# Hashed attention and two MLPs on one core: hash in 32-column tiles, bits through DRAM, values in threes

## The chip, the cores and the metric

One core of one Trainium2 chip. The metric is the device time of one execution in microseconds (us). The engines are named as in the profile: PE (TensorE matmul), PEld (its weight loads), DVE (VectorE), ACT (ScalarE), POOL (GpSimd) and SP (SyncE, which here only issues DMAs).

## The reference

Sixteen heads (2 x 8) of 768 queries and keys, 64 features each. A query attends to a key only where six sign bits of a projection agree. Two MLPs follow (1536 tokens, 512 to 2048 to 512).

```python
q_bits = (np.einsum('bhsd,dk->bhsk', q, proj) > 0)      # k_bits alike, 6 bits
mask = q_bucket[:, :, :, None] == k_bucket[:, :, None, :]
scores = np.where(mask, scale * np.matmul(q, k.transpose(0, 1, 3, 2)), -1e9)
attn = np.exp(scores - max); attn = attn / (sum + 1e-9)
x = np.matmul(attn, v)                                  # then to 1536 x 512
h = x @ w_in;  g = softplus(h);  x = g @ w_out          # MLP 1
h = x @ w_in;  g = h * clip(h + 3, 0, 6) / 6;  out = g @ w_out   # MLP 2
```

## The kernel before

The program is written by a planner (`Schedule`). Each `plan.add` names an operation, its planned cost on each engine that may run it, the buffers it reads and writes, and a priority (lower goes first). `Schedule.run` then plays the program forward on a model of the engines: at each step it takes the engine whose next operation would end first, and gives that engine the operation with the lowest priority among those that can start soonest. The order in which it emits the instructions is the order in which each engine's queue executes them on the chip. So every constant of the planner (`TH`, `WHEN`, `STAY`, `START`, `EVERY`, `STEP`, `PROJECT`, `ACTIVATE`, `FETCH`, `AHEAD`) changes only orders, and the choice of engine where an operation may run on two.

`prepare(h)` loads a head and builds its operands. The tile `raw` holds k on partitions 0 to 63 and q on 64 to 127. `qa`, `ka` are rounded parts, `qb`, `kb` the remainders (64 rows) with 32 rows of bits below them (`KB` = 96): q's bits and ones, k's bits and -2^33, so that the product of `qb` and `kb` also counts bit mismatches as a large penalty. `dot` (L379) multiplies `raw` by the signed projection `hashes`, in two matmuls of 64 output columns and 384 keys that stand side by side in the array, into one PSUM bank `d`; L401 compares it with 0 on all 128 partitions (`bt`, 128x384), and four DMAs (L410) carry 32 rows each from `bt` to `qb` and `kb`. For head 0, DVE writes the bits to `qb`/`kb` itself (L391, four instructions of 32 rows).

`attend(h)` runs six query blocks `t`. For each: four score matmuls (L437 with `qa`/`ka`, L438 with `qb`/`kb`) into a two-bank PSUM tile `sc`; the maximum over keys on DVE (L451); a tiny DVE instruction that makes bias and scale (L458); exp on ACT with a row sum (L466); six PE transposes to `tp` (L477), and their copy to `et` (L249 on ACT or L251 on DVE; DVE may have it where `t % 3` is 0). `sc` and `tp` share three two-bank tiles. The product with v (`some(c)`, L493) has six key blocks `c`, each two 64-column matmuls side by side; they are planned as three operations of two blocks. Each such fp32 matmul stands in the trace as two instructions, so a head has 24 rows of L493 and 4 of L379. `xa`, `pt` (L515), `xn`, and per two heads `xt` (L557), `xh`, `xl` bring the result to the MLP's layout. `d`, `av`, `pt` and `xt` share two single PSUM banks ("av", "pre"). During attention one block of MLP weights per head is also converted from 64-bit floats, on ACT and DVE (L600 to L643); its earliest start is `START + EVERY * n`.

The MLPs (L662 hidden, L755/L757 output) are 2304 matmuls of 512 columns on PE.

Of the kernel before, what the change touches and what calls it, by code (L numbers as in the profile page):

```python
# [9 lines left out]
F32 = mybir.dt.float32  # L10
# [21 lines left out]
LATER = 4  # L32
BITS = 3
EX = 3

TH = 16.41
WHEN = dict(load_p=-69.22, load_k=-58.24, load_q=23.18, load_v=-47.14, high_k=64.04, high_q=79.83, low_k=32.38, low_q=105.41, copy_q=116.1, dots=124.52, bits=46.23, send=11.13, scores=-1.98, max=-149.65, exp=-149.76, turn=-8.77, even=-56.85, values=53.65, back=58.37, rec=72.46, norm=75.82, x=27.98, x_high=21.57, x_low=7.85)
# [11 lines left out]
STEP = 8.253  # L49
PROJECT = 11.022  # L50
ACTIVATE = -66.584
FETCH = 125.921
AHEAD = -20.863


def f32(ap):
# [28 lines left out]
class Schedule:  # L85
# [24 lines left out]
    def run(self):  # L110
        free = dict(A=1.96, D=0.1, P=0.6, T=0.1, S=0.65, H=0.0, G=0.0, M=0.0)
        lanes, busy, mode = [0.0] * LANES, {}, "r"
        ready = {op: self.times(op) for op in self.ops if not op.open}
        while ready:
            options = []
            for op, times in ready.items():
                slot = self.slots(op)
                if slot is not None:
                    for e, t in times.items():
                        at, end, unit = max(free[e], slot, t), op.cost[e], e  # L120
                        if e == "T":
# [5 lines left out]
                        options.append((op.prio, at, at + end, unit, e, op))  # L127
# [8 lines left out]
            _, start, end, _, e, op = min(rivals, key=lambda o: (late(o), o[1]))  # L136
# [24 lines left out]
        assert all(op.done is not None for op in self.ops)  # L161
        return max(free.values())
# [30 lines left out]
def lsh_attention_two_mlps(  # L193
# [37 lines left out]
    for name in ("x", "w", "bits"):  # L231
        open_pool(name, ctx)
    open_pool("ps", ctx, space=PSUM)
    open_pool("tail", attention, side="right")
    open_pool("heads", heads)

# [26 lines left out]
    thr = buffer("heads", [P, 1], F32, "thr", 1, "thr")  # L263
    top = buffer("heads", [P, 1], F32, "top", 1, "top")

    def set_rows(e):

        for u in range(P // ROWS):
            bounds = ((0.0, NB), (-TINY, NR), (0.0, P)) if u % 2 == 0 else ((-TINY, NB), (0.0, P))
            rows = thr.ap[u * ROWS : (u + 1) * ROWS, :]  # L270
            for i, (value, _) in enumerate(bounds):
                if i == 0:
                    nc.gpsimd.memset(rows, value)
                else:
                    nc.gpsimd.affine_select(
                        out=rows, in_=rows, compare_op=ALU.is_gt, fill=value, base=bounds[i - 1][1],
                        pattern=[[0, 1]], channel_multiplier=-1,
                    )
            nc.gpsimd.memset(top.ap[u * ROWS : (u + 1) * ROWS, :], -BIG if u % 2 else 1.0)
# [17 lines left out]
    plan.add(dict(D=0.6), set_hashes, reads=[p32], writes=[hashes], prio=-39)  # L297


    qa, qb, ka, kb, vx = {}, {}, {}, {}, {}  # L300

    def prepare(h):
        at = h * TH
# [77 lines left out]
                    start=True, stop=True,  # L381
                )

        plan.add(dict(T=0.646), dot, mode="c", reads=[raw, hashes], writes=[dots], prio=at + WHEN["dots"])
        if h == 0:
            for u in range(2):
                for n, x in enumerate((qb, kb)):
                    rows = slice((2 * u + n) * ROWS, (2 * u + n + 1) * ROWS)
                    plan.add(
                        dict(D=0.6),  # L390
                        lambda e, u=u, x=x, rows=rows: nc.vector.tensor_scalar(  # L391
                            x[h].ap[D:KB, u * HALF : (u + 1) * HALF], dots.ap[rows, :HALF], thr.ap[rows, 0:1],
                            top.ap[rows, 0:1], op0=ALU.is_gt, op1=ALU.mult,
                        ),
                        reads=[dots, thr, top], writes=[x[h]], prio=at + WHEN["bits"],
                    )
            return
        bits = buffer("heads", [P, HALF], F32R, "bt", 2, f"bt{h}")
        plan.add(
            dict(D=0.585),  # L400
            lambda e: nc.vector.tensor_scalar(  # L401
                bits.ap, dots.ap[:, :HALF], thr.ap[:, 0:1], top.ap[:, 0:1], op0=ALU.is_gt, op1=ALU.mult
            ),
            reads=[dots, thr, top], writes=[bits], prio=at + WHEN["bits"],
        )
        for u in range(2):
            for n, x in enumerate((qb, kb)):
                plan.add(
                    queue,
                    lambda e, u=u, n=n, x=x: engines[e].dma_start(  # L410
                        out=f32(x[h].ap[D:KB, u * HALF : (u + 1) * HALF]),
                        in_=f32(bits.ap[(2 * u + n) * ROWS : (2 * u + n + 1) * ROWS, :]),
                    ),
                    reads=[bits], writes=[x[h]], prio=at + WHEN["send"], dma=(0.2, 1.95),
                )


    xn = {}
# [1 line left out]
    def attend(h):  # L420
# [19 lines left out]
        for t in range(NT):  # L440
# [3 lines left out]
            for u in range(2):  # L444
                last_scores = plan.add(
                    dict(T=0.353), lambda e, sc=sc, t=t, u=u: scores(sc, t, u),
                    reads=[qa[h], qb[h], ka[h], kb[h]], writes=[sc], prio=step + WHEN["scores"],
                )
            plan.add(
                dict(D=0.866),  # L450
                lambda e, sc=sc, t=t: nc.vector.reduce_max(  # L451
                    nm.ap[:, t, 0:1], sc.ap[:, :, :HALF], axis=AX.XY, negate=True
                ),
                reads=[sc], writes=[nm], prio=step + WHEN["max"],
            )
            plan.add(
                dict(D=0.07),
                lambda e, t=t: nc.vector.scalar_tensor_tensor(  # L458
                    bs.ap[:, t, :], nm.ap[:, t, 0:1].to_broadcast([P, 2]), 0.5 * BIG, nm.ap[:, t, :],
                    op0=ALU.is_lt, op1=ALU.mult,  # L460
                ),
                reads=[nm], writes=[bs], prio=step + WHEN["max"],
            )
# [17 lines left out]
            def even(e, tp=tp, t=t):  # L481
# [399 lines left out]
```

## Time and profile before

| | |
|---|---|
| time, median of 3 | 787.0 us (785.72 to 787.37) |
| profiled execution: its own time | 787.35 us |
| its span, first to last instruction | 785.6 us |
| granted PE clock, mean | 0.998 |
| busy: PE, PEld, DVE, ACT | 764.9, 599.1, 529.0, 485.0 us |

A matmul row's length runs to the modelled end of its pipeline and overlaps the next; the distance between the starts of neighbouring rows is the time that PE gives to each. A row of the chain is time on the path that ended last.

### The profile page before, as it was taken

How to read it: one execution, taken by the hardware profiler on the slowest of the kernel's cores; microseconds unless marked ns; L12 is line 12 of the kernel's file. 1: busy time of each engine (PE TensorE's matmuls, PEld its weight loads, DVE VectorE, ACT ScalarE, POOL GpSimd, SP SyncE). 2: the span in 40 equal slices, each digit the busy share in tenths (PEclk: the TensorE clock that was granted, in tenths of full speed). 3: DMA queues.
4: the chain of work that ended last, by engine and by line, in shares of the span. 5: the costliest groups of instructions: out<-in, count | busy, mean ns of one | idle time of the engine just before them, and what ended most of it. 6: DMA issues, size and time to landing. Idle time of an engine off the chain costs nothing.

```text
span 785.6 us, 10356 instructions
## 1 busy us (share of the span) xinstructions
PE 764.9 (97%) x3808; PEld 599.1 (76%) x3808; DVE 529.0 (67%) x938; ACT 485.0 (62%) x821; POOL 9.5 (1%) x53
## 2 busy tenths in 40 slices
PE   4999999999999999999999999999999999999997
PEld 2677677677668788878888788878888888888886
DVE  6698887888986999964545899999932222232222
ACT  3789999998988778665556678766622322232222
POOL 1000000000000000000000000000000000000000
PEclk9999999999999999999999999999999999999999
DMA  5354454353323070000000555530000100010001
GB/s 165 108 162 116 115 165 120 110 163 118 80 73 134 28 294 1 1 0 1 1 0 1 188 196 191 177 107 1 1 0 14 42 0 1 1 53 1 1 0 54
DMA packets 26354, 58.61 MB, mean 75 GB/s; under 512 B 3584, under 2 KB 7552, under 8 KB 26304
## 3 DMA queue, kind: packets, MB, share of 16 engines
q1 hardware_dynamic: 22128, 49.56, 19.7%
q10 hardware_dynamic: 4176, 8.39, 3.4%
q8 instruction: 30, 0.49, 0.3%
q14 instruction: 20, 0.16, 0.1%
HBM read 48.89 MB, written 3.15 MB: 66 GB/s over the span
## 4 chain that ended last, share of the span: by engine, by line
PE 90%; ACT 4%; DVE 3%; issue 2%; DMA 1%; SPq 0%; ACTq 0%; DVEq 0%
PE ph L662 34%; PE acc L755 17%; PE acc L757 17%; PE tp L477 7%; PE av L493 6%; PE sc L437 4%; PE sc L438 3%; ACT e L466 2%; DVE nm L451 2%; PE xt L557 1%; ACT ka L249 1%; PE pt L515 1%; PE d L379 1%; DMA raw<-in_q_dram 1%; ACT et L249 0%
## 5 line engine op out<-in xcount | busy, mean ns | idle before, releaser
L662 PE MATMUL ph<-xh,w 128*128 128x512 f32 x768 | 239.1, 393 | 0.0
L662 PEld LDWEIGHTS ph<-xh,w 128*128 128x128 f32 x768 | 143.8, 188 | 31.7
L662 PE MATMUL ph<-xl,w 128*128 128x512 f32 x384 | 150.2, 391 | 0.0
L691 DVE SCALAR_TENSOR_TENSOR ml<-me,ph 128x512 f32<-128x512 f32 x48 | 33.1, 690 | 116.0 <-ACT me L686 115.8
L686 ACT ACTIVATE me<-ph,three 128x512 f32<-128x512 f32 x48 | 33.0, 687 | 124.2 <-PE ph L662 120.7
L466 ACT ACTIVATE e<-sc,bs 128x768 f32<-128x768 f32 x96 | 94.0, 986 | 19.0 <-DVE bs L458 19.0
L451 DVE TENSOR_REDUCE nm<-sc 128x1 f32<-128x768 f32 x96 | 88.7, 951 | 20.8 <-PE sc L438 20.6
L755 PE MATMUL acc<-gh,w 128*128 128x512 f32 x384 | 98.8, 395 | 0.1
L757 PE MATMUL acc<-w,gh 128*128 128x512 f32 x384 | 97.4, 392 | 0.0
L477 PEld LDWEIGHTS tp<-ident,e 128*128 128x128 f32 x576 | 63.3, 142 | 29.3 <-ACT e L466 20.2
L755 PEld LDWEIGHTS acc<-gh,w 128*128 128x128 f32 x384 | 70.9, 188 | 19.1 <-ACT gh L249 2.8
L757 PEld LDWEIGHTS acc<-w,gh 128*128 128x128 f32 x384 | 72.1, 188 | 16.2
L662 PEld LDWEIGHTS ph<-xl,w 128*128 128x128 f32 x384 | 72.1, 188 | 16.0
L477 PE MATMUL tp<-ident,e 128*128 128x128 f32 x576 | 76.6, 281 | 4.9 <-ACT e L466 3.8
L437 PE MATMUL sc<-ka,qa 128*128 128x384 f32 x192 | 69.1, 360 | 0.1
L493 PE MATMUL av<-et,vx 128*64 128x384 f32 x384 | 68.8, 494 | 0.0
L438 PE MATMUL sc<-kb,qb 96*128 96x384 f32 x192 | 65.3, 340 | 0.8 <-DVE kb L391 0.7
L249 ACT ACTIVATE et<-tp 128x768 f32<-128x768 f32 x82 | 62.2, 815 | 2.4 <-PE tp L477 2.3
L722 DVE SCALAR_TENSOR_TENSOR me<-mu,me 128x512 f32<-128x512 f32 x48 | 33.3, 693 | 33.1 <-ACT mu L717 33.0
L249 ACT ACTIVATE gh<-ml 128x512 fp32r<-128x512 f32 x48 | 30.2, 629 | 38.8 <-DVE ml L734 38.6
L755 PE MATMUL acc<-gl,w 128*128 128x512 f32 x192 | 53.4, 392 | 0.7 <-ACT xh L249 0.7
L757 PE MATMUL acc<-w,gl 128*128 128x512 f32 x192 | 53.1, 391 | 0.0
(65 smaller groups left out, 957.8 us busy)
## 6 DMA issues: line engine op xcount, KB each, us to landing
raw<-in_moe_w_out_dram SPq DMA_DIRECT2D x30, 512.0 KB, 3.5
raw<-in_moe_w_in_dram SPq DMA_DIRECT2D x18, 512.0 KB, 4.3
raw<-in_moe_w_in_dram ACTq DMA_DIRECT2D x14, 512.0 KB, 4.8
rawk<-in_kv_dram SPq DMA_DIRECT2D x15, 384.0 KB, 5.0
raw<-in_kv_dram SPq DMA_DIRECT2D x16, 192.0 KB, 3.2
raw<-in_q_dram SPq DMA_DIRECT2D x16, 192.0 KB, 3.7
vx<-in_kv_dram SPq DMA_DIRECT2D x16, 192.0 KB, 3.0
out_dram<-y SPq DMA_DIRECT2D x12, 256.0 KB, 2.1
```

The lines of the kernel that those rows point to most:

```text
L249: nc.scalar.activation(out, in_, AF.Copy)
L437: nc.tensor.matmul(o, qa[h].ap[:, qs], ka[h].ap[:, cs], start=True, stop=False)
L438: nc.tensor.matmul(o, qb[h].ap[0:KB, qs], kb[h].ap[0:KB, cs], start=False, stop=True)
L451: lambda e, sc=sc, t=t: nc.vector.reduce_max(nm.ap[:, t, 0:1], sc.ap[:, :, :HALF], axis=AX.XY, negate=True),
L466: lambda e, sc=sc, ex=ex, t=t: nc.scalar.activation(ex.ap.rearrange("p (u k) -> p u k", u=2), sc.ap[:, :, :HALF], AF.Exp, bias=bs.ap[:, t, ...
L477: nc.tensor.transpose(o, ex.ap[:, c * P : (c + 1) * P], ident.ap)
L493: nc.tensor.matmul(av.ap[u * D : (u + 1) * D, :HALF], vx[h].ap[:, c, :], et[u].ap[:, c, :], start=(c == 0), stop=(c == NT - 1),)
L662: nc.tensor.matmul(bank(), w[:, a, :], x[b].ap[:, kc, :], start=(kc + i == 0), stop=(kc == KC - 1 and i == 2))
L691: lambda e: nc.vector.scalar_tensor_tensor(l.ap, e1.ap, 6.0, bank(), op0=ALU.min, op1=ALU.mult),
L722: lambda e: nc.vector.scalar_tensor_tensor(e1.ap, u.ap, -1.0, e1.ap, op0=ALU.add, op1=ALU.subtract),
L755: nc.tensor.matmul(o, w.ap[:, a, cs], b.ap, start=st, stop=sp)
L757: nc.tensor.matmul(o, b.ap[:, cs], w.ap[:, a, :], start=st, stop=sp)
```

## The change

- The hash of heads 1 to 15 is four matmuls (`dot4`) of 32 output columns and 192 keys, one for each quarter of the keys, side by side, with `hash4` as weights. The comparison is one instruction on 128x192 (planned 0.386 for 0.585), with threshold columns `thr4`, `top4` of its own. The bit rows in `qb` and `kb` shrink from 32 to 16 (`KB` = 80).
- The bits go to `qb` and `kb` through a DRAM tile `sent`: one DMA writes it, two read it (before: four DMAs within SBUF).
- Head 0 keeps the old hash; its four bit writes are four planned operations in the order q0, k0, k1, q1, and a score matmul waits only for the halves that it reads.
- POOL builds `thr4`, `top4` (28 small instructions) and `hash4` (three) at the start.
- Maximum and bias of a query block are one planned operation, so L458's successor follows its maximum at once on DVE.
- The copy of `tp` may go to DVE for every `t`.
- The products with v are two planned operations of three key blocks (before: three of two).
- The planner adds `LEAN` (0.731 us) to DVE's end when it compares engines for an operation that two may run, and `LOOK`: an operation of lower priority number may be taken although it can start only up to 0.412 us (ACT), 0.103 (DVE) or 0.108 (PE) later than the soonest one.
- All constants have new values.

```diff
-TH = 16.41
+GROUP = 3
+TH = 14.059
-STAY = 10.971
+STAY = 48.452
+LEAN = 0.731
+LOOK = dict(A=0.412, D=0.103, T=0.108)
-START, EVERY = 33.82, 14.426
+START, EVERY = 19.12, 13.251
...
-            end, unit = min((o[2], o[3]) for o in options)
+            end, unit = min((o[2] + o[6], o[3]) for o in options)
...
-            rivals = [o for o in rivals if o[1] <= soon]
+            rivals = [o for o in rivals if o[1] <= soon + LOOK.get(unit, 0.0)]
...
-    KB = D + ROWS
+    BR = ROWS // 2
+    KB = D + BR
+    QT = S // 4
...
+    def set_quarters(e):
+        for u in range(P // ROWS):
+            rows = slice(u * ROWS, (u + 1) * ROWS)
+            steps(thr4.ap[rows, :], ((0.0, NB), (-TINY, NR), (0.0, BR), (-TINY, BR + NB), (0.0, P)))
+            steps(top4.ap[rows, :], ((1.0, BR), (-BIG, P)))
+    plan.add(dict(P=1.2), set_quarters, writes=[thr4, top4], prio=4)
...
+    def set_hash4(e):
+        nc.gpsimd.memset(hash4.ap, 0.0)
+        for n in range(2):
+            nc.gpsimd.tensor_copy(hash4.ap[:, n * BR : n * BR + NR], hashes.ap[:, n * ROWS : n * ROWS + NR])
...
+        def dot4(e):
+            for u in range(4):
+                nc.tensor.matmul(
+                    dots.ap[u * ROWS : (u + 1) * ROWS, :QT], hash4.ap, raw.ap[:, u * QT : (u + 1) * QT],
+                    start=True, stop=True,
+                )
...
-        bits = buffer("heads", [P, HALF], F32R, "bt", 2, f"bt{h}")
+        plan.add(dict(T=0.36), dot4, mode="c", reads=[raw, hash4], writes=[dots], prio=at + WHEN["dots"])
+        bits = buffer("heads", [P, QT], F32R, "bt", 2, f"bt{h}")
...
-        for u in range(2):
-            for n, x in enumerate((qb, kb)):
-                plan.add(
-                    queue,
-                    lambda e, u=u, n=n, x=x: engines[e].dma_start(
...
+        sent = buffer("rows", [4, 2, BR, QT], F32, "sent", 2, f"sent{h}")
+        plan.add(
+            queue,
+            lambda e: engines[e].dma_start(out=sent.ap.rearrange("u n r c -> (u n r) c"), in_=f32(bits.ap)),
+            reads=[bits], writes=[sent], prio=at + WHEN["send"], dma=(0.4, 2.1),
+        )
+        for n, x in enumerate((qb, kb)):
+            plan.add(
+                queue,
+                lambda e, n=n, x=x: engines[e].dma_start(
+                    out=f32(x[h].ap[D:KB, :]).rearrange("r (u c) -> r u c", u=4),
+                    in_=sent.ap[:, n].rearrange("u r c -> r u c"),
...
+            def bias(e, sc=sc, t=t):
+                nc.vector.reduce_max(nm.ap[:, t, 0:1], sc.ap[:, :, :HALF], axis=AX.XY, negate=True)
+                nc.vector.scalar_tensor_tensor(
...
+            plan.add(dict(D=0.935), bias, reads=[sc, nm], writes=[bs], uses=[nm], prio=step + WHEN["max"])
...
-                dict(A=0.692) if t % 3 else dict(A=0.692, D=0.867), even, reads=[tp], writes=[et[t // n]], prio=step + WHEN["even"],
+                dict(A=0.692, D=0.867), even, reads=[tp], writes=[et[t // n]], prio=step + WHEN["even"],
...
-        for c in range(0, NT, 2):
+        for c in range(0, NT, GROUP):
...
-                    dict(T=1.29), mode="c", emit=lambda e, c=c: [some(c), some(c + 1)],
+                    dict(T=0.645 * GROUP), mode="c", emit=lambda e, c=c: [some(c + i) for i in range(GROUP)],
```

## Rows read from the trace of the kernel before

**Rows 1.** Windows: busy us of each engine by stretch (x instructions), clock, DMA.
```profile
0.00:40.00 40.00, 28.28 (x153) 19.09 (x154) 26.99 (x49) 24.09 (x39) 2.81 (x25) 0.96 0.49 135
...
98.40:127.60 29.20, 28.52 (x191) 20.87 (x190) 24.83 (x49) 27.21 (x48) 1.02 (x4) 1.00 0.44 131
...
244.40:320.00 75.60, 75.60 (x345) 59.42 (x344) 71.49 (x133) 57.62 (x102) 0.08 (x1) 1.00 0.28 107
320.00:520.00 200.00, 199.93 (x867) 161.67 (x866) 147.79 (x249) 133.71 (x226) 0.00 (x0) 1.00 0.24 82
```

**Rows 2.** Chain of work that ended last, 98.4 to 127.6 us, share by line.
```profile
by line: PE tp L477 25.6%; PE av L493 23.7%; PE sc L437 14.6%; PE sc L438 13.9%; issue 6.6%; ACT e L466 6.0%; PE d L379 3.0%; PE xt L557 2.7%; ACT ka L249 2.4%; PE pt L515 2.3%
```

**Rows 3.** Timeline of PE, 105 to 128 us: start, length, line, tile, xcount [idle before].
```profile
105.39 2.18 PE L477 MATMUL tp<-ident,e 128*128 128x128 f32 x18
107.33 0.42 PE L437 MATMUL sc<-ka,qa 128*128 128x384 f32 x1
...
109.63 1.51 PE L493 MATMUL av<-et,vx 128*64 128x384 f32 x8
110.97 0.81 PE L379 MATMUL d<-raw,hash 128*64 128x384 f32 x4
111.72 2.55 PE L477 MATMUL tp<-ident,e 128*128 128x128 f32 x18
114.02 0.42 PE L437 MATMUL sc<-ka,qa 128*128 128x384 f32 x1
...
116.24 0.49 PE L515 MATMUL pt<-ident,xa 128*128 128x128 f32 x3
116.66 2.80 PE L493 MATMUL av<-et,vx 128*64 128x384 f32 x16
119.39 1.53 PE L477 MATMUL tp<-ident,e 128*128 128x128 f32 x12
120.76 0.60 PE L557 MATMUL xt<-ident,xn 128*128 128x128 f32 x4
121.19 0.82 PE L477 MATMUL tp<-ident,e 128*128 128x128 f32 x6
...
124.41 1.51 PE L493 MATMUL av<-et,vx 128*64 128x384 f32 x8
126.50 0.87 PE L379 MATMUL d<-raw,hash 128*64 128x384 f32 x4 [0.58 <-PE av L493]
127.30 0.87 PE L477 MATMUL tp<-ident,e 128*128 128x128 f32 x6
```

**Rows 4.** Timeline of DVE and ACT where a maximum, its bias and exp stand.
```profile
115.63 1.81 DVE L451 TENSOR_REDUCE nm<-sc 128x1 f32<-128x768 f32 x2
117.36 0.28 DVE L458 SCALAR_TENSOR_TENSOR bs<-nm 128x2 f32<-128x2 f32 x2
117.56 0.95 DVE L451 TENSOR_REDUCE nm<-sc 128x1 f32<-128x768 f32 x1
...
117.63 0.99 ACT L466 ACTIVATE e<-sc,bs 128x768 f32<-128x768 f32 x1 [0.99 <-DVE bs L458]
...
125.98 0.41 DVE L254 TENSOR_TENSOR xl<-xt,xh 128x256 fp32r<-128x256 f32 x1
```

**Rows 5.** Waits, 40 to 230 us: engine line <- releaser: us in total, times, longest.
```profile
PEld tp L477 <- ACT e L466: 15.8, 31, 1.0
...
ACT e L466 <- DVE bs L458: 11.2, 10, 2.0
...
PE d L379 <- PE av L493: 2.3, 4, 0.6
```

**Rows 6.** Groups of instructions: busy us, mean ns of one | idle before (0 to 280 us).
```profile
L249 ACT ACTIVATE et<-tp 128x768 f32<-128x768 f32 x82 | 62.2, 815 | 2.4 <-PE tp L477 2.3
...
L251 DVE COPY et<-tp 128x768 f32<-128x768 f32 x14 | 13.2, 944 | 0.0
L401 DVE TENSOR_SCALAR bt<-d,thr,top 128x384 fp32r<-128x384 f32 x15 | 10.0, 665 | 0.0
```

**Rows 7.** Tile bt's DMAs; then SP's queue and PE for head 9; a DRAM write.
```profile
L410 SPq DMA_DIRECT2D qb<-bt x30: 512/580/589, 12.9 to 213.3; - x30
L410 SPq DMA_DIRECT2D kb<-bt x30: 507/582/590, 13.5 to 214.7; - x30
...
DMA to landing us min/median/max: 1.9/1.9/5.1
...
124.51 0.54 SPq L410 DMA_DIRECT2D qb<-bt  x1
126.99 0.51 SPq L410 DMA_DIRECT2D kb<-bt  x1
...
143.49 0.34 PE L438 MATMUL sc<-kb,qb 96*128 96x384 f32 x1
...
out_dram<-y SPq DMA_DIRECT2D x12, 256.0 KB, 2.1
```

**Rows 8.** Timeline of the start: DVE's bits of head 0, PE, POOL.
```profile
0.99 0.42 POOL L275 TENSOR_SCALAR_AFFINE_SELECT thr<-thr 32x1 f32<-32x1 f32 x2
1.36 0.09 POOL L279 MEMSET top<- 32x1 f32 x1
3.32 0.29 POOL masks.py:199 TENSOR_SCALAR_AFFINE_SELECT ident<-ident 128x128 f32<-128x128 f32 x1
7.44 2.83 PE L379 MATMUL d<-raw,hash 128*64 128x384 f32 x8 [7.44 <-DVE hash L295]
10.08 0.67 DVE L391 TENSOR_SCALAR kb<-d,thr,top 32x384 fp32r<-32x384 f32 x1
10.20 0.69 PE L437 MATMUL sc<-ka,qa 128*128 128x384 f32 x1
11.49 0.69 DVE L391 TENSOR_SCALAR kb<-d,thr,top 32x384 fp32r<-32x384 f32 x1
12.23 0.45 PE L438 MATMUL sc<-kb,qb 96*128 96x384 f32 x1 [0.75 <-DVE kb L391]
17.12 3.71 PE L477 MATMUL tp<-ident,e 128*128 128x128 f32 x18 [2.24 <-ACT e L466]
```

More of the change, by code (lines that the diff above doesn't have):

```diff
@@ L34 @@
 EX = 3
-TH = 16.41
-WHEN = dict(load_p=-69.22, load_k=-58.24, load_q=23.18, load_v=-47.14, high_k=64.04, high_q=79.83, low_k=32.38, low_q=105.41, copy_q=116.1, dots=124.52, bits=46.23, send=11.13, scores=-1.98, max=-149.65, exp=-149.76, turn=-8.77, even=-56.85, values=53.65, back=58.37, rec=72.46, norm=75.82, x=27.98, x_high=21.57, x_low=7.85)
+GROUP = 3
+TH = 14.059
+WHEN = dict(load_p=-184.9, load_k=-188.62, load_q=94.89, load_v=90.47, high_k=132.71, high_q=-248.04, low_k=-31.51, low_q=153.42, copy_q=-85.55, dots=135.85, bits=-47.41, send=309.07, scores=-60.36, max=-59.07, exp=-81.4, turn=-146.4, even=-32.01, values=-27.91, back=8.35, rec=-79.64, norm=-33.72, x=-77.14, x_high=-149.93, x_low=-30.15)
 CROSS = dict(TA=0.2, TD=0.2, TS=0.2, AT=0.16, AD=0.135, AS=0.12, AP=0.19, DA=0.16, DT=0.15, DS=0.1, PD=0.15, ST=0.1, SA=0.1, SD=0.1)
@@ L43 @@
 SWITCH = dict(rt=0.0, rc=0.138, tr=0.007, tc=0.145, cr=0.205, ct=0.156)
-STAY = 10.971
+STAY = 48.452
 ISSUE, SETUP, LANDED = 0.6, 1.3, 0.4
 LANES = 8
+LEAN = 0.731
+LOOK = dict(A=0.412, D=0.103, T=0.108)
 TICK, WARM = 3.413, 0.374
-START, EVERY = 33.82, 14.426
[L49 to L53, printed above, removed]
+START, EVERY = 19.12, 13.251
+STEP = 20.832
+PROJECT = 25.193
+ACTIVATE = 61.059
+FETCH = 328.932
+AHEAD = -88.98
 def f32(ap):
@@ L126, in run @@
                             at, end, unit = max(at, free["G"], lanes[-LANES]), ISSUE, "G"
-                        options.append((op.prio, at, at + end, unit, e, op))
+                        options.append((op.prio, at, at + end, unit, e, op, LEAN if e == "D" and len(op.cost) > 1 else 0.0))
             if not options:
                 raise RuntimeError("no operation can go on")
-            end, unit = min((o[2], o[3]) for o in options)
+            end, unit = min((o[2] + o[6], o[3]) for o in options)
             rivals = [o for o in options if o[3] == unit]
             soon = min(o[1] for o in rivals)
-            rivals = [o for o in rivals if o[1] <= soon]
+            rivals = [o for o in rivals if o[1] <= soon + LOOK.get(unit, 0.0)]
             late = lambda o: o[0] + (STAY if unit == "T" and o[5].mode != mode else 0.0)
-            _, start, end, _, e, op = min(rivals, key=lambda o: (late(o), o[1]))
+            _, start, end, _, e, op, _ = min(rivals, key=lambda o: (late(o), o[1]))
             cost = op.cost[e] if op.dma else end - start
@@ L233, in lsh_attention_two_mlps @@
     open_pool("ps", ctx, space=PSUM)
+    open_pool("rows", ctx, space=bass.MemoryType.DRAM)
     open_pool("tail", attention, side="right")
@@ L264, in lsh_attention_two_mlps, with steps @@
     top = buffer("heads", [P, 1], F32, "top", 1, "top")
+    thr4 = buffer("heads", [P, 1], F32, "thr4", 1, "thr4")
+    top4 = buffer("heads", [P, 1], F32, "top4", 1, "top4")
+    def steps(rows, bounds):
+        for i, (value, _) in enumerate(bounds):
+            if i == 0:
+                nc.gpsimd.memset(rows, value)
+            else:
+                nc.gpsimd.affine_select(
+                    out=rows, in_=rows, compare_op=ALU.is_gt, fill=value, base=bounds[i - 1][1],
+                    pattern=[[0, 1]], channel_multiplier=-1,
+                )
     def set_rows(e):
         for u in range(P // ROWS):
[L269 to L279, printed above, removed]
+            rows = slice(u * ROWS, (u + 1) * ROWS)
+            steps(thr.ap[rows, :], ((0.0, NB), (-TINY, NR), (0.0, P)) if u % 2 == 0 else ((-TINY, NB), (0.0, P)))
+            nc.gpsimd.memset(top.ap[rows, :], -BIG if u % 2 else 1.0)
+    def set_quarters(e):
+        for u in range(P // ROWS):
+            rows = slice(u * ROWS, (u + 1) * ROWS)
+            steps(thr4.ap[rows, :], ((0.0, NB), (-TINY, NR), (0.0, BR), (-TINY, BR + NB), (0.0, P)))
+            steps(top4.ap[rows, :], ((1.0, BR), (-BIG, P)))
     plan.add(dict(P=0.9), set_rows, writes=[thr, top], prio=-3)
+    plan.add(dict(P=1.2), set_quarters, writes=[thr4, top4], prio=4)
     p32 = buffer("heads", [P, NB], F32, "p32", 1, "p32")
@@ L297, in lsh_attention_two_mlps @@
     plan.add(dict(D=0.6), set_hashes, reads=[p32], writes=[hashes], prio=-39)
+    hash4 = buffer("heads", [P, ROWS], F32, "hash4", 1, "hash4")
+    def set_hash4(e):
+        nc.gpsimd.memset(hash4.ap, 0.0)
+        for n in range(2):
+            nc.gpsimd.tensor_copy(hash4.ap[:, n * BR : n * BR + NR], hashes.ap[:, n * ROWS : n * ROWS + NR])
+    plan.add(dict(P=0.4), set_hash4, reads=[hashes], writes=[hash4], prio=4)
     qa, qb, ka, kb, vx = {}, {}, {}, {}, {}
+    parts = {}
     def prepare(h):
@@ L382, in dot @@
                 )
-        plan.add(dict(T=0.646), dot, mode="c", reads=[raw, hashes], writes=[dots], prio=at + WHEN["dots"])
+        def dot4(e):
[4 more added lines that the diff above has]
+                )
         if h == 0:
+            plan.add(dict(T=0.646), dot, mode="c", reads=[raw, hashes], writes=[dots], prio=at + WHEN["dots"])
             for u in range(2):
                 for n, x in enumerate((qb, kb)):
-                    rows = slice((2 * u + n) * ROWS, (2 * u + n + 1) * ROWS)
-                    plan.add(
+                    rows = slice((2 * u + n) * ROWS, (2 * u + n) * ROWS + BR)
+                    parts[n, u] = plan.add(
                         dict(D=0.6),
@@ L394, in prepare @@
                         ),
-                        reads=[dots, thr, top], writes=[x[h]], prio=at + WHEN["bits"],
+                        reads=[dots, thr, top], writes=[x[h]], prio=at + WHEN["bits"] + (u if n else 5 * u),
                     )
             return
-        bits = buffer("heads", [P, HALF], F32R, "bt", 2, f"bt{h}")
+        plan.add(dict(T=0.36), dot4, mode="c", reads=[raw, hash4], writes=[dots], prio=at + WHEN["dots"])
+        bits = buffer("heads", [P, QT], F32R, "bt", 2, f"bt{h}")
         plan.add(
-            dict(D=0.585),
+            dict(D=0.386),
             lambda e: nc.vector.tensor_scalar(
-                bits.ap, dots.ap[:, :HALF], thr.ap[:, 0:1], top.ap[:, 0:1], op0=ALU.is_gt, op1=ALU.mult
+                bits.ap, dots.ap[:, :QT], thr4.ap[:, 0:1], top4.ap[:, 0:1], op0=ALU.is_gt, op1=ALU.mult
             ),
-            reads=[dots, thr, top], writes=[bits], prio=at + WHEN["bits"],
+            reads=[dots, thr4, top4], writes=[bits], prio=at + WHEN["bits"],
         )
-        for u in range(2):
-            for n, x in enumerate((qb, kb)):
-                plan.add(
-                    queue,
-                    lambda e, u=u, n=n, x=x: engines[e].dma_start(
[L411 to L415, printed above, removed]
+        sent = buffer("rows", [4, 2, BR, QT], F32, "sent", 2, f"sent{h}")
[3 more added lines that the diff above has]
+            reads=[bits], writes=[sent], prio=at + WHEN["send"], dma=(0.4, 2.1),
+        )
+        for n, x in enumerate((qb, kb)):
[4 more added lines that the diff above has]
+                    in_=sent.ap[:, n].rearrange("u r c -> r u c"),
+                ),
+                reads=[sent], writes=[x[h]], prio=at + WHEN["send"], dma=(0.3, 2.5),
+            )
     xn = {}
@@ L446, in attend @@
                     dict(T=0.353), lambda e, sc=sc, t=t, u=u: scores(sc, t, u),
-                    reads=[qa[h], qb[h], ka[h], kb[h]], writes=[sc], prio=step + WHEN["scores"],
-                )
[L449 to L458, printed above, removed]
+                    reads=[qa[h], ka[h]], writes=[sc], uses=[qb[h], kb[h]], prio=step + WHEN["scores"],
+                    after=[
+                        op for i, x in enumerate((qb[h], kb[h])) for op in x.writers
+                        if op not in parts.values() or op is parts[i, (t // n, u)[i]]
+                    ],
+                )
+            def bias(e, sc=sc, t=t):
+                nc.vector.reduce_max(nm.ap[:, t, 0:1], sc.ap[:, :, :HALF], axis=AX.XY, negate=True)
+                nc.vector.scalar_tensor_tensor(
                     bs.ap[:, t, :], nm.ap[:, t, 0:1].to_broadcast([P, 2]), 0.5 * BIG, nm.ap[:, t, :],
                     op0=ALU.is_lt, op1=ALU.mult,
-                ),
-                reads=[nm], writes=[bs], prio=step + WHEN["max"],
-            )
+                )
+            plan.add(dict(D=0.935), bias, reads=[sc, nm], writes=[bs], uses=[nm], prio=step + WHEN["max"])
             plan.add(
```

## Prediction

> **What bounds the kernel now.** I read the windows by stage first [rows 1]. From 320 us on PE is busy 199.93 of 200 us; that is the MLPs, 2304 matmuls that the change does not touch. The stretch before it, 244 to 320 us, has PE busy throughout too, with DVE at 71.49 of 75.6 us. So the gain or loss must arise in the attention part, which a pattern of two heads fills: 29.20 us with 191 matmul rows, DVE busy 24.83 and ACT 27.21 us. That is two engines near their end at once: PE shows 28.52 us, but as rows overlap, its starts are needed to tell work from waits; ACT has 2.0 us left.
>
> The chain of the same two heads [rows 2] is on PE for some 86%; ACT's exp has 6.0%, the rounding of k 2.4%, "issue" 6.6%. A PE instruction saved there is on the path, as long as ACT (93% busy) does not take over.
>
> The timeline of PE [rows 3] then gives work and waits. By the distance between starts: values of two key blocks 1.34 us (109.63 to 110.97), values of four blocks 2.73 (116.66 to 119.39), hash 0.75 (110.97 to 111.72), 18 transposes 1.94 when nothing holds them (105.39 to 107.33), three query blocks of scores 2.22 to 2.30 (114.02 to 116.24, 107.33 to 109.63). Two places are longer: the second hash starts 2.09 us after its values begin, where 1.34 is the work, so 0.75 us are a wait; the transposes at 111.72 take 2.30, so 0.36 is a wait.
>
> **The change part by part.** *The hash.* Before, its four rows take 0.75 us: two side-by-side pairs in series (the values, of the same form, take 1.34 for four pairs, 0.33 each, so 0.65 for two) and about 0.10 us for leaving the 64-column mode. Half the columns make a pair's pass half as long, and four tiles stand side by side where two did: 0.33 + 0.10 = 0.43 us, 0.32 saved. Times 15 heads: -4.8 us. Four tiles side by side are not in this trace. Bounds: full overlap as for two tiles, -4.8; none, eight rows of half a pair's 0.33, 1.3 + 0.10 = 1.4 us, so +0.65 x 15 = +9.8. I take the lower end, since the pair shows no loss at all [rows 3].
>
> *A new change of mode.* In both heads of rows 3 the hash stands directly behind values and shares their mode; now it has 32-column tiles and they 64. Leaving a mode costs about 0.10 us by the hash's own sum above. If the hash keeps its place, that is 15 x 0.10 = +1.5 us; if it moves away from the values, it makes an entry and an exit of its own, about twice that, +3.0. I take +1.5. The Trainium skill (TensorEngine Tiling (Array Packing), Key Properties) says that changing the tiling mode, not just the tile, drains TensorE; this is the rule that speaks against the change, and the 0.10 us agrees with it. The planner's cost of 0.36 us knows nothing of it.
>
> *The wait of the hash.* At 126.50 the hash waits until the DVE instruction `xl` at 125.98, 0.41 long, has read the bank that it will write [rows 3, 4]. It happens in 4 places [rows 5], 0.75 us each by the starts, 3.0 us in all. New priorities reorder both; nothing in the trace says that they leave the hash clear of the two shared banks. Bounds 0 and -3.0; I take half, -1.5.
>
> *Maximum and bias as one step.* Rows 4 show what it removes: two maxima run back to back (115.63 to 117.36), and only then both biases, so the first exp of three, at 117.63, has waited 0.99 us although its maximum was there about 0.87 us earlier. Exp waits for its bias 11.2 us in 10 places between 40 and 230 us, and weight loads of transposes wait for exp 15.8 us, mostly under cover of running matmuls [rows 5]. What of it reaches PE is the 0.36 us above, once in two heads, 2.7 us in 15 heads. Bounds: 0, if the exp's end is set by ACT's other work, and -4 with the start's; I take -1.5. It adds no instruction.
>
> *Values in threes.* No instruction is saved. In rows 3 the three planned groups already stand as 4 + 2 blocks, two visits to the 64-column mode a head; two groups of three need two visits as well. 0, between -3 (one visit a head saved, 2 x 0.10 us x 15) and +3 (the hash apart from both).
>
> *Copies on either engine.* ACT does 82 of 96 at 815 ns, DVE 14 at 944 [rows 6], though DVE was allowed 32. The old limit did not bind by number, only by place. The new freedom lets ACT give up some when PE gets shorter; no gain by itself, and `LEAN` keeps them mostly on ACT. The comparison `bt` falls from 665 ns [rows 6] to nearly half plus overhead, some 0.4: 0.27 us of DVE a head, hidden, since DVE has 4.4 us of idle time in two heads [rows 1].
>
> *Bits through DRAM.* All 60 old sends were on SP's queue, issue 0.58 us, median landing 1.9 us [rows 7]. New: three issues instead of four, but the two reads wait on the queue for the write to land; loads of later heads and the copy of q stand behind them. A DRAM write of 256 KB lands in 2.1 us [rows 7], so the route takes about 4 us instead of 2. Its cover: head 9's sends are issued at 124.51 to 126.99 and first read by PE at 143.49, over 11 us after any landing, and the write need not wait for `qb` to be free. I cost it at 0; without the cover it would be about 2 us a head. On ACT's queue the wait for the write would stop ACT, up to 2 us a head; of the 60 sends that were free to go there, none did.
>
> *The start.* The second score product waits 0.75 us for the fourth bit write of head 0 [rows 8]; with the order q0, k0, k1 it comes one DVE instruction of 0.67 us earlier: -0.7. POOL's 28 new instructions, at about 0.15 us each (those from 0.99 to 1.36 and on), 4.5 us in all, push `ident` from 3.3 to about 8 us; its first user is at 17.12 [rows 8]. `hash4` comes after, at 9 to 10 us, and head 1's hash with it; PE is waiting for head 0's bits until 10.2 anyhow. 0, at worst +0.5.
>
> *The MLPs.* 0: PE is full there; new priorities only reorder. With DVE at 95% between 244 and 320 us there is little room for a better order, and a worse one would show as PE idle time; I allow -1 to +2.
>
> Sum: -4.8 + 1.5 - 1.5 - 1.5 - 0.7 = -7.0 us. Against the profiled execution's 787.35 that is 780.35; the median is 0.35 lower, so **780.0 us**. A pair of heads becomes about 28.3 us. ACT's 27.2 us still fits (96%).
>
> **The rivals.** *A: the waits go altogether.* The unstalled pieces of rows 3 for two heads: transposes 4 x 1.94, scores 4 x 2.25, values 2 x (2.73 + 1.34), hash 2 x (0.43 + 0.10), `pt` 2 x 0.42, `xt` about 0.63 = 27.4 us. So 29.2 - 27.4 = 1.8 us per pair, 7.5 pairs, and the start: -14.2, **773**. For it: each wait has a cause in the order alone. Against: ACT's 27.2 us would be 99% of it, so copies must go to DVE as well.
>
> *B: ACT becomes the bound.* PE's savings turn into waits for exp; only the start gains: **786**. For: ACT at 93%. Against: DVE's 4.4 us per pair, and the new freedom to use them.
>
> *C, slower: the four tiles do not overlap.* +9.8 in place of -4.8, the rest as forecast: +7.6, **795**. It makes the kernel slower as soon as the four tiles take over about 0.9 us together. For: no row shows four. The Trainium skill (TensorE: Matmul & The Clock Gate, Part 3) gives 2.38 times for three column tiles; by that, as an estimate, four would lose a quarter and the hash would save 1 or 2 us less.
>
> *D, slower: deliberate holes.* `LOOK` lets ACT stay idle up to 0.41 us for a more urgent operation. Twelve exps per pair, one hole before each: 4.9 us, against 2.0 us left on ACT. It decides from five holes per pair on; with eight, +1.3 us x 7.5 = +10, less the start, dots being no help then: **796**. Against: the order is all that the chip sees, and a hole planned before an exp is filled on the chip if its data come earlier.
>
> **How the numbers follow.** Forecast (776 to 785) 0.50, A 0.22, B 0.12, C 0.07, D 0.09. A change within 0.2% (1.6 us) is about what cannot be told from none. Faster by more: forecast and A, less the forecast's upper edge, 0.71; same: B and that edge, 0.13; slower: C and D, 0.16. The range reaches down past A by its bound for the bias (-4, so 771), and up over B by the worst of the unknown costs (mode entry +1.5, POOL +0.5), 788.5; C and D are left out.
>
> **What would show it.** Hash: eight rows of 192 columns, starts a few ns apart in fours, about 0.43 us to the next row; right behind values 0.1 more. Right for the bias: L451 and L458 strictly by turns, and ACT's wait for L458 well below 11 us. Right for the start: the second L438 0.7 us earlier. A pair of heads of 28.3 us (27.4 by A, 29.2 by B and above by D). SP's reads land over 5 us before L438 reads them. Wrong, if PE waits for exp as much as it saved, if the hash's rows stand 0.16 us apart, or if PE idles after 245 us.

## The result and the profile after

The change made the kernel slower: 797.0 us (median of four) against 786.4 us, a ratio of 1.0139 (95% interval 1.0125 to 1.0152). The profiled span is 795.0 us.

The windows of the changed kernel, with the columns of [rows 1]:

```profile
0.00:40.00 40.00, 26.97 (x178) 19.39 (x179) 28.18 (x52) 25.66 (x41) 10.14 (x57) 1.00 0.56 165
...
127.60:156.80 29.20, 28.74 (x196) 20.15 (x195) 28.66 (x52) 26.24 (x46) 1.04 (x4) 1.00 0.43 126
156.80:186.00 29.20, 28.59 (x197) 20.50 (x197) 28.63 (x55) 26.62 (x47) 0.74 (x5) 1.00 0.46 133
...
244.40:320.00 75.60, 74.58 (x330) 57.11 (x330) 72.32 (x129) 55.61 (x94) 0.00 (x0) 1.00 0.24 95
320.00:520.00 200.00, 196.39 (x842) 156.59 (x841) 140.88 (x231) 131.61 (x217) 0.00 (x0) 1.00 0.24 77
```

Two things differ from [rows 1]. In attention DVE is busy 28.6 of 29.2 us, where it was 24.83. Between 98.4 and 215.2 us it has not one wait of over 0.15 us for another engine; in the kernel before, the same view (engine line <- releaser: total us, times, longest) has these:

```profile
DVE nm L451 <- PE sc L438: 7.5, 7, 2.2
DVE xl L254 <- ACT xh L249: 6.9, 4, 1.8
```

So DVE has no room left. And in the MLPs PE, which was full, fits fewer matmuls into the same time: 330 for 345 and 842 for 867, 40 rows, at about 0.23 us each some 9 us.

Where the time went, in us from the span's start, read from the timeline of PE (starts of the first score matmul of heads 2 and 12, end of the last transposes of attention by their last start, start of the last matmul), with the kernels of the experiments below:

| kernel | time | head 2 | head 12 | per head | last transpose | last matmul |
|---|---|---|---|---|---|---|
| before | 786.4 | 41.53 | 187.23 | 14.57 | 245.53 | 780.88 |
| after | 797.0 | 40.77 | 186.70 | 14.59 | 243.78 | 790.24 |
| a_pairs | 792.7 | 40.80 | 186.73 | 14.59 | 243.82 | 786.04 |
| a_bias_free | 787.0 | 39.79 | 178.96 | 13.92 | 233.84 | 780.30 |
| a_bias_later | 804.7 | 41.58 | 192.10 | 15.05 | 250.70 | 797.15 |
| a_copies_act | 794.8 | 40.64 | 184.62 | 14.40 | 240.54 | 788.11 |
| b_hash4 | 786.4 | 41.77 | 186.11 | 14.43 | 244.50 | 780.30 |
| b_bias_now | 788.1 | 39.88 | 187.54 | 14.77 | 246.10 | 781.28 |
| c_joined | 779.9 | 41.20 | 180.62 | 13.94 | 239.85 | 772.64 |

In its first 40 us the profiled run of the kernel before had a granted clock of 0.96 [rows 1], all others of the table 1.00; by 0.04 of PE's 28.28 busy us its times are late by an estimated 1.1 us. The distances from head 2 on are not touched by that.

A head takes as long as before, although PE has less to do in it; and the part from the last transpose to the last matmul has grown from 535.4 to 546.5 us. So by place the loss is that of the MLPs, 11.1 us, and of the 7.0 us forecast for attention and start little came: the last transpose is 1.8 us earlier, some 0.7 without the difference in clock.

The hash itself did what it should. PE's timeline of the changed kernel; the rows of before are in [rows 3]:

```profile
137.24 2.16 PE L532 MATMUL av<-et,vx 128*64 128x384 f32 x12
139.33 0.53 PE L415 MATMUL d<-raw,hash 128*32 128x192 f32 x8
139.79 1.53 PE L516 MATMUL tp<-ident,e 128*128 128x128 f32 x12
```

From its start to the next row the hash takes 0.46 us (it took 0.75), so the four tiles run side by side.

PE's waits of the changed kernel up to 240 us, then from 235 us on (engine line <- releaser: total us, times, longest):

```profile
...
PE d L415 <- POOL hash L324: 3.9, 1, 3.9
PE tp L516 <- ACT e L505: 3.6, 10, 1.1
...
PE acc L794 <- ACT xh L255: 4.2, 6, 0.7
PE acc L794 <- ACT gh L255: 1.6, 5, 0.4
```

Before, the second stretch had a single such wait, of 0.7 us. The hash's wait for its bank [rows 5] is gone; a wait for POOL stands at the start. And ACT's wait for the bias from 40 to 230 us, which the joined step was to bring well below 11.2 us [rows 5], has grown:

```profile
ACT e L505 <- DVE bs L497: 12.1, 16, 2.2
```

### The profile page after: what moved, and what is told of

Same layout as the page of the kernel before. It is cut to its first block, busy times and chain, and to the rows that moved or that the text cites. A ratio compares the mean times of both kernels' runs of the same rounds, so it can differ in the third digit from the quotient of the medians.

```text
span 795.0 us, 10521 instructions
## 1 busy us (share of the span) xinstructions
PE 768.1 (97%) x3868; PEld 595.2 (75%) x3868; DVE 554.5 (70%) x958; ACT 481.9 (61%) x801; POOL 16.7 (2%) x84
## 4 chain that ended last, share of the span: by engine, by line
PE 64%; DVE 24%; issue 4%; ACT 3%; DMA 3%; POOL 1%; SPq 0%; DVEq 0%; POOLq 0%; ACTq 0%
PE ph L701 26%; PE acc L796 17%; PE acc L794 10%; DVE nm L496 4%; PE tp L516 4%; PE av L532 3%; DVE bits L665 3%; DVE bits L672 2%; PE sc L479 2%; DVE w L260 2%; PE sc L480 2%; ACT e L505 2%; DVE me L769 2%; DVE me L761 2%; DVE bits L658 1%
## 5 line engine op out<-in xcount | busy, mean ns | idle before, releaser
L496 DVE TENSOR_REDUCE nm<-sc 128x1 f32<-128x768 f32 x96 | 91.2, 950 | 5.0 <-PE sc L480 4.6
L480 PE MATMUL sc<-kb,qb 80*128 80x384 f32 x192 | 65.7, 342 | 0.0
L255 ACT ACTIVATE et<-tp 128x768 f32<-128x768 f32 x62 | 48.2, 811 | 4.7 <-PE tp L516 4.3
```

The source lines that it names most:

```text
L255: nc.scalar.activation(out, in_, AF.Copy)
L480: nc.tensor.matmul(o, qb[h].ap[0:KB, qs], kb[h].ap[0:KB, cs], start=False, stop=True)
L496: nc.vector.reduce_max(nm.ap[:, t, 0:1], sc.ap[:, :, :HALF], axis=AX.XY, negate=True)
```

## The experiments

Theories: (1) DVE has become the bound of attention, because more copies were put on it and because a bias right behind its maximum must wait for it; (2) the start is late because of POOL; (3) the MLPs lose time at the ends of token groups by an order in which PE waits for ACT. The rival to all: the new order is slower for other reasons, such as the holes of `LOOK`. A name with a_ is an edit of the changed kernel, with b_ of the kernel before, in both cases with every other instruction in its planned place, unless it is said that the plan was made anew.

**The MLPs.** `a_pairs` issues the matmuls of a bank pair's second column ahead of ACT's copy of the first:

```diff
-lambda e, i=i, cs=cs: [some(i, c) for c in cs],
+lambda e, i=i, cs=cs: [some(i, c) for c in cs] if len(cs) > 1 else (
+    [] if cs[0] % 2 else [some(i, cs[0])] + ([some(k, cs[0] + 1) for k in range(3)] if i == 2 else [])
+),
```

> The changed kernel with the same planned order; at the end of each token group of an MLP the three matmuls of the second column block of a two-bank PSUM tile are issued in the program before ACT's copy of the first block (before, one of them stood behind that copy and waited for it). PE's own order is the same. MLP theory: six such waits of 0.69 us plus the restart go, and PE idles less at 341 to 345, 432 to 436 and 524 to 528 us: 792 to 793.5 us against 797.0. Rival: the copies start later instead and the next group's matmuls wait for them: 796 to 797.5 us.

Measured: 792.7 us, 4.4 below the changed kernel. A group end in the timeline of the changed kernel, PE and ACT:

```profile
341.51 0.63 PE L794 MATMUL acc<-gh,w 128*128 128x512 f32 x2
342.18 0.60 ACT L255 ACTIVATE xh<-acc 128x512 fp32r<-128x512 f32 x1 [0.56 <-PE acc L794]
342.83 0.50 PE L794 MATMUL acc<-gl,w 128*128 128x512 f32 x1 [0.69 <-ACT xh L255]
```

The same place in PE's timeline of a_pairs:

```profile
341.57 0.63 PE L794 MATMUL acc<-gh,w 128*128 128x512 f32 x2
342.04 0.39 PE L794 MATMUL acc<-gl,w 128*128 128x512 f32 x1
```

The third matmul of the second column waited for ACT to read the first: the two columns are different banks of one tile, and an order in the program between a read and a write of one tile becomes a wait. Theory 3 holds for 4.4 us.

`b_mlp_new` gives the kernel before the five MLP constants of the changed one (`STEP`, `PROJECT`, `ACTIVATE`, `FETCH`, `AHEAD`).

> The kernel before with nothing changed but the five constants that order the MLPs (STEP, PROJECT, ACTIVATE, FETCH, AHEAD), which take the values of the changed kernel. If these constants cause the loss after 244 us, the part behind the last scores grows by some 6 to 9 us, with waits of PE for ACT's xh at the group ends: 792 to 795 us against 786.4. Rival: the loss comes from what the attention part leaves to be done (conversions, the rules LEAN and LOOK): 786 to 787.5 us.

Measured: 787.9 us, ratio 1.0015 (1.0006 to 1.0024): the constants alone cost about 1 us, far from 792 to 795 and just above the rival's range. One wait for `xh` at a group end stands in its trace, as in before's. So the six waits of the changed kernel do not come from these constants alone; which other part of its plan brings them was not tried.

**The start.** `a_hash4_dve` fills `hash4` on DVE:

```diff
-        nc.gpsimd.memset(hash4.ap, 0.0)
+        nc.vector.memset(hash4.ap, 0.0)
...
-            nc.gpsimd.tensor_copy(hash4.ap[...], hashes.ap[...])
+            nc.vector.tensor_copy(hash4.ap[...], hashes.ap[...])
```

> The changed kernel, its order of work untouched, except that the three small instructions that fill hash4 are issued on DVE instead of POOL. Start theory: the first hash of head 1 stood behind POOL's 28 instructions (PE waited 3.9 us for them) and pushed the first scores from 10.2 to 12.9 us; with DVE the first scores come at 10.3 to 10.7 us and the whole takes 794.3 to 795.0 us instead of 797.0. Rival: from 40 us on DVE is full and sets the pace, so a later start is swallowed: first scores earlier, time 796.5 to 797.3.

Measured: 796.6 us. The first scores come at 8.96 instead of 12.90 us, but head 2's at 40.50 instead of 40.77: the rival is right, 3.9 us of start are swallowed within two heads. What POOL did in the changed kernel, with two rows of DVE:

```profile
6.63 0.95 DVE L260 TENSOR_TENSOR kb<-raw,ka 64x768 fp32r<-64x768 f32 x1
6.77 2.32 POOL L280 TENSOR_SCALAR_AFFINE_SELECT thr<-thr 32x1 f32<-32x1 f32 x4
7.60 0.95 DVE L373 SCALAR_TENSOR_TENSOR qa<-raw,qa 64x768 fp32r<-64x768 f32 x1
...
9.58 0.94 POOL L280 TENSOR_SCALAR_AFFINE_SELECT thr<-thr 32x1 f32<-32x1 f32 x4
...
11.73 0.32 POOL L324 COPY hash<-hash 128x12 f32<-128x12 f32 x2
```

**The bias.** `b_bias_now` issues, in the kernel before, each bias right behind its maximum.

```diff
 lambda e, sc=sc, t=t: (nc.vector.reduce_max(nm.ap[:, t, 0:1], sc.ap[:, :, :HALF], axis=AX.XY, negate=True),
+    nc.vector.scalar_tensor_tensor(bs.ap[:, t, :], ...)),
...
-lambda e, t=t: nc.vector.scalar_tensor_tensor(bs.ap[:, t, :], ...),
+lambda e: None,
```

> The kernel before with its planned order untouched, and only the bias instruction issued right behind its maximum (96 of them, before often after a second maximum). Forecast of this step: exps start up to 0.87 us earlier, 785 us (range 783 to 786.4). DVE theory: each maximum then takes 0.11 us longer to the next instruction, 0.7 us a head, which DVE's 4.4 us of idle time in two heads can hide here: 785.5 to 787 us, with 0.98 us from a maximum to its bias in the trace. It speaks against both if the time grows beyond 789.

Measured: 788.1 us, ratio 1.0022 (1.0012 to 1.0032). I had forecast this step to be faster; it is 2 us slower, and a head takes 0.20 us more. That is also 1 us above the range of the DVE theory: the wait costs time even where DVE has room. Where in a head it is lost was not followed.

`a_bias_later` does the reverse in the changed kernel: the bias is issued one DVE instruction after its maximum.

```diff
+            held = list(LATE)
             op.emit(e)
+            if e == "D":
+                now(held)
...
-                nc.vector.scalar_tensor_tensor(
+                LATE.append(lambda: nc.vector.scalar_tensor_tensor(
```

> The changed kernel with the same planned order, except that the tiny bias instruction is issued on DVE one DVE instruction after its maximum instead of right behind it (or just ahead of its exp, if that is issued first). DVE theory: in the changed kernel DVE is busy 28.6 of 29.2 us per pair of heads, and the bias that reads its maximum at once stretches the distance from a maximum to the next instruction from 0.87 to 0.98 us; 0.11 us for some 72 maxima between 40 and 215 us go, 789 to 792 us. Rival: the order of PE and ACT sets the pace, and exps that now wait 0.3 to 0.9 us longer for their bias cost as much: 796 to 800 us.

Measured: 804.7 us, above both ranges. The direction is the rival's: ACT waits for biases 15.7 us between 98 and 215 us, where it waited 9.5. The run doesn't speak on DVE's load, as it adds a delay to each exp while it takes one from DVE. It needed an edit that moves nothing. `a_bias_free` computes the bias from a constant tile:

```diff
-bs.ap[:, t, :], nm.ap[:, t, 0:1].to_broadcast([P, 2]), 0.5 * BIG, nm.ap[:, t, :],
+bs.ap[:, t, :], still.ap[:, 0:1].to_broadcast([P, 2]), 0.5 * BIG, still.ap,
```

> The changed kernel with the same planned order and the same instructions, but the bias of each query block is computed from a constant tile (-1, 1) instead of the maximum that DVE has just written (the maximum is still taken; softmax loses only its shift, and rows that match no key come out differently). So the bias keeps its place right behind the maximum and loses only its dependence on it. Theory of the dependent bias: DVE is full between 40 and 215 us, the distance from a maximum to its bias falls from 0.98 to 0.87 us, 0.7 us a head: a head takes 13.9 us instead of 14.59, the whole 787.5 to 789.5 us. Rival (PE's and ACT's order sets the pace, as the delayed bias that made it slower may say): a head stays at 14.4 to 14.6 us, the whole at 795.5 to 797.

Measured: 787.0 us, 10.0 below the changed kernel. DVE's timeline in the changed kernel:

```profile
129.46 0.95 DVE L496 TENSOR_REDUCE nm<-sc 128x1 f32<-128x768 f32 x1
130.44 0.16 DVE L497 SCALAR_TENSOR_TENSOR bs<-nm 128x2 f32<-128x2 f32 x1
130.52 0.95 DVE L496 TENSOR_REDUCE nm<-sc 128x1 f32<-128x768 f32 x1
```

The same three instructions in a_bias_free:

```profile
124.85 0.95 DVE L504 TENSOR_REDUCE nm<-sc 128x1 f32<-128x768 f32 x1
125.72 0.15 DVE L505 SCALAR_TENSOR_TENSOR bs<-still 128x2 f32<-128x2 f32 x1
125.79 0.95 DVE L504 TENSOR_REDUCE nm<-sc 128x1 f32<-128x768 f32 x1
```

The rows are equally long, but the bias that reads the maximum starts 0.98 us after it, the other 0.87. With 6 maxima, 0.11 us each is 0.66 us a head, and a head falls from 14.59 to 13.92: by just that. The chain of work that ended last, from 98 to 127 us by line, is on PE alone in a_bias_free:

```profile
by line: PE av L540 33.0%; PE tp L524 30.8%; PE sc L487 14.9%; PE sc L488 14.5%; PE d L423 3.2%; PE xt L604 2.3%; PE pt L562 2.2%
```

Theory 1 holds for attention, and there the rival falls: `LOOK` and the order are the same in both. The part from the last transpose to the last matmul is 546.5 us in both, so the run says nothing on the MLPs' loss. It leaves out the softmax's shift by the maximum, and so shows what the wait costs; it is no replacement.

**The copies.** `a_copies_act` brings the old rule back (DVE only for `t % 3` of 0), planned anew with all constants kept; `a_copies_pairs` adds the two mends of a_hash4_dve and a_pairs.

> The changed kernel planned again with the old rule for the copies of tp (DVE only where t % 3 is 0; 17 on DVE instead of 34, the others on ACT); all else and all constants as in the changed kernel. Theory that DVE is full because of copies and dependent biases: DVE gets about 1 us a head back, ACT has room for it, 13.9 to 14.4 us a head and 789 to 795 us. Rival (the new order is slower for other reasons than DVE's load): 797 or more. If the copies alone were at fault, it would be 786 or less.

> As a_copies_act, with the two mends that touch no order: hash4 filled by DVE, and both columns of a bank pair written before either is read at the group ends. If the causes add, it is 4.4 to 5 us below a_copies_act, 785 to 790 us.

Measured: 794.8 and 791.0 us. Half of DVE's 34 copies, most of what had come to it, were worth 2.2 us and 0.2 us a head, with the order that the new plan gave to the rest; the mends 3.9 more, a little less than forecast. The copies are a part of DVE's load, but not the larger one.

**The hash.** `b_hash4` puts hash, thresholds, 128x192 comparison and the route through DRAM into the kernel before:

```diff
+            if h:
+                for u in range(4):
+                    nc.tensor.matmul(dots.ap[u * ROWS : (u + 1) * ROWS, :QT], quarter["hash4"], raw.ap[:, u * QT : (u + 1) * QT], ...)
+                return
```

> The kernel before with its planned order untouched, and only the hash of heads 1 to 15 changed: four tiles of 32 columns, the comparison on 128x192, the bits by one DMA to DRAM and two from there; hash4 is filled by DVE and the thresholds by POOL behind the identity matrix. Forecast of this step: -4.8 us for the hash and +1.5 for the extra change of mode, and the route through DRAM hidden: 783.1 us against 786.4 (range 781.5 to 785). Rival 1: the four tiles do not overlap, 795. Rival 2: the pace is set by ACT in this order, so that PE's savings become waits: 786 to 786.8.

Measured: 786.4 us beside 786.0, ratio 1.0005 (0.9996 to 1.0014). PE's timeline of it, to be laid beside 109.63 to 111.72 in [rows 3]:

```profile
109.30 1.51 PE L540 MATMUL av<-et,vx 128*64 128x384 f32 x8
110.75 0.53 PE L411 MATMUL d<-raw,hash 128*32 128x192 f32 x8
111.21 1.76 PE L524 MATMUL tp<-ident,e 128*128 128x128 f32 x12
```

The values take 1.45 us instead of 1.34, the hash 0.46 instead of 0.75: 0.18 us saved, and a head gets 0.14 shorter. From head 2 to the last transpose that is 1.3 us, yet the whole is not faster: head 2 comes 0.2 us later than before, although the clock of these first 40 us is 1.00 here and 0.96 there. The number is that of rival 2, but its reason is not: PE's waits from 40 to 230 us are 3.0 us here and 2.9 before. What the start of b_hash4 loses was not followed further. The DMAs of `sent` land in 2.0 us at the median.

**All mends, and the costs put right.** `a_three` joins a_hash4_dve, a_bias_later and a_pairs.

> The changed kernel with three mends at once, its planned order untouched: hash4 by DVE, the bias one DVE instruction later, the bank pairs of the group ends written before they are read. If the three causes (start, DVE's dependent bias, MLP group ends) are separate, the gains add: 797.0 less 2.5, 5 to 8 and 4 is 782 to 786 us, not slower than the kernel before. Rival: each mend only uncovers the next wait, 790 to 795 us.

Measured: 799.0 us, above both ranges: it is about a_bias_later less the gains of a_pairs and a_hash4_dve, so the mend of the bias makes it slower here too.

`c_joined` is the changed kernel with the mends of a_hash4_dve and a_pairs (the latter as a planned order), the costs below, and all constants searched again:

```diff
-SAME = dict(A=0.13, D=0.05, ...)
+SAME = dict(A=0.13, D=0.12, ...)
-plan.add(dict(D=0.935), bias, ...)
+plan.add(dict(D=1.07), bias, ...)
-narrow = dict(D=0.93)
+narrow = dict(D=0.98)
-plan.add(dict(P=1.2), set_quarters, ...)
+plan.add(dict(P=7.9), set_quarters, ...)
```

`c_apart` is the same with maximum and bias as two planned operations.

> The changed kernel with the planner's costs put right by what the runs showed (maximum with bias 1.07 us instead of 0.935, 0.12 instead of 0.05 us between dependent DVE instructions, remainder of q 0.98, POOL's thresholds 7.9), hash4 filled by DVE, both columns of a bank pair written before either is read, and the constants searched again with these costs. If the wrong costs were the cause, the chip now follows the plan: 13.9 us a head, 779 to 782 us, faster than the kernel before (786.4) by 0.6 to 0.9%. Rival (the plan's model fails in other ways, too): 785 or more.

> As c_joined, but maximum and bias are two planned operations again, so that another DVE instruction may stand between them, with constants of a search of its own (values one key block at a time). Its plan is 1.2 us longer than that of c_joined: 780 to 783.5 us by the same theory; if the model fails in other ways, 785 or more.

Measured: c_joined 779.9 us, ratio 0.9923 (0.9906 to 0.9939); c_apart 782.8, 0.9958 (0.9943 to 0.9973). Both beat both kernels. The windows of c_joined:

```profile
127.60:156.80 29.20, 29.20 (x208) 20.97 (x204) 27.83 (x52) 27.84 (x49) 0.70 (x4) 1.00 0.51 148
...
244.40:320.00 75.60, 75.43 (x338) 59.34 (x335) 73.67 (x136) 57.24 (x99) 0.00 (x0) 1.00 0.22 84
320.00:520.00 200.00, 199.80 (x866) 161.65 (x866) 145.93 (x246) 134.03 (x224) 0.00 (x0) 1.00 0.26 85
```

DVE and ACT share the work evenly (27.8 us each), PE is full at 208 rows, and the MLPs are full again. It keeps the maximum with its bias, at 13.94 us a head, with 29 copies on DVE. The costs came together with the two mends and a new search, so their own share is not shown by these runs.

## Why the prediction was wrong

I forecast 780.0 us with a range up to 788.5 (its terms add up to 788.3), which left out the slower rivals C and D, and 0.16 for slower. Two terms of the sum failed, the joined bias and the MLPs, each by more than the whole gain of 7.0 us that I forecast. Step by step:

- *Maximum and bias as one step* (-1.5, "it adds no instruction"): failed. I counted instructions, and not the distance between a maximum and an instruction that reads it. 0.11 us times 96 is 10.6 us, and 10.0 were measured. The trace of before had it: two maxima ahead of two biases hide a part of the wait (1.93 us of DVE for two query blocks, 115.63 to 117.56 in [rows 4], against 2 x 1.06 in the changed kernel, 129.46 to 130.52 above), and from the maximum at 117.56 to an instruction that doesn't read it are 0.87 us:

```profile
118.43 0.55 DVE L530 TENSOR_TENSOR xn<-pt,rec 128x384 f32<-128x384 f32 x1
118.89 0.15 DVE L458 SCALAR_TENSOR_TENSOR bs<-nm 128x2 f32<-128x2 f32 x1
```

- *Copies on either engine* ("no gain by itself", LEAN keeping them on ACT): wrong. ACT kept 62 of 96 and DVE had 34 instead of 14. Half of these were worth 2.2 us. I checked ACT's room for shorter heads (27.2 of 28.3 us) and never DVE's after the change: 24.83 us, 2.2 for 20 copies in eight pairs at 0.87, 1.3 for the biases, less 0.5 for the comparison, is 27.8 of 28.3, or 98%.
- *The MLPs* (0, -1 to +2, "PE is full there; new priorities only reorder"): failed, and by place it is the larger miss, 11.1 us. A full PE was a property of the old order; the new one opened waits. 4.4 us are the group ends (a_pairs). 6.9 of the growth remain in a_pairs. MLP matmuls start 0.23 us apart as a rule; the longer distances hold 2.8 us of lost time before, 12.5 in the changed kernel and 8.0 in a_pairs, there half of it at waits of output matmuls for `gh` (2.5 us idle in 7 places). From before to a_pairs that is 5.2 of the 6.9; another 1.4 are six MLP matmuls that start ahead of the last transpose in the kernel before, and none in the changed one. Which choice of the plan makes these two was not tried.
- *The hash* (-4.8, +1.5): right in its sizes, 0.29 and 0.11 us a head, for 0.32 and 0.10. The rows start 7 ns apart in fours, so rival C falls, and so does the quarter that its estimate from three tiles would have lost. That PE's time is then worth its size was wrong: with DVE full it shows nowhere, and even in the old order the whole got no faster (b_hash4).
- *The hash's wait* (-1.5): all of it went, and it too went into a chain that DVE set.
- *The start* (-0.7; POOL +0.5 at worst): POOL's new work ended at 12.0 us and not 9 to 10, PE waited 3.9 us; two heads later 0.3 us were left of it.
- *Bits through DRAM* and *values in threes* (0): right; the reads for head 8 land at 118.9 us, 9 us ahead of its first scores, and none lands less than 5.0 us ahead. The chain of the changed kernel from 98 to 186 us does pass through `sent` (3.3%) and the loads of k that stand behind it on SP's queue (7.7%), but without a wait of DVE there; with DVE relieved it is on PE alone.
- *Rival D*'s 796 is luck: no hole before an exp is needed, since a_bias_free keeps `LOOK` and gains its 10 us. Rival B named the right kind of thing, an engine that becomes the bound, but the other engine.

A bound per engine after the change, not before it, would have shown the first of the two failed terms: the time of a step that is on no path can put its engine on one.

The Trainium skill (VectorE: DVE Perf Modes, The DRAIN you can't avoid) reports that eight chained copies took as long with a semaphore after each as with one after the last, so that the semaphore costs nothing extra there. For this pair the trace differs: 0.98 us to an instruction that depends on the one before it and waits for its semaphore, 0.87 to the same instruction without both; the measurement decides.

What the planner had believed can be worked out from its own arithmetic: it gives 777.0 us for the program before and 766.4 for the changed one, a gain of 10.6. If both orders are kept and only the costs listed with c_joined are put in, it gives 777.9 and 782.6. The old order has slack where its costs are too low; the changed one was searched with the same errors, and puts work exactly where the table is too cheap. The 4.7 us between them are not the whole loss: the waits that a_pairs removes, a write behind a read of the same tile, are not in the planner's model.

## What to carry over

When a change moves work to an engine that has room, add up that engine's time after the change, with distances from start to start and with the wait of an instruction on the one just before it. Two dependent instructions fused into one planned step lose the place where another could hide that wait; c_joined, which keeps the fused step, is faster than both kernels with the wait in its cost table. That an engine is full is a reading of one order, and no reason to put the next order's term there at nothing. A search over a cost table finds the table's errors first: before trusting its gain, replay its order with durations measured in the trace.

## What the runs showed of the hardware

The bias, on 128x2, starts 0.98 us after a maximum over 768 columns that it reads (0.975 to 0.995 for all 96 in the changed kernel), and 0.87 us after it where it does not read it (median of 96 in a_bias_free). Of the four small selects on POOL that took 2.32 us from 6.77 us, the first two took 0.86 and 0.90 us and end within 0.1 us of DVE's two instructions of 6.63 and 7.60 us, each of which reads two tiles; the four from 9.58 us took 0.18 each. That DVE's instructions are the reason was not tried. Eight rows of 192 columns in four 32-column tiles take 0.46 us with the exit from their mode, and values that change to that mode 0.11 us more.
